# An attention and feed-forward kernel on one core: another order of the same 782 steps

## The chip, the core and the metric

The kernel runs on one core of a Trainium2 chip. The metric is the device time of one execution in microseconds; smaller is better. The core's engines work side by side and each takes its own instructions in program order: PE (TensorE: matmuls, with its weight loads listed as PEld), DVE (VectorE), ACT (ScalarE), POOL (GpSimd) and SP (SyncE, used here to issue transfers). They wait for each other through semaphores. Transfers are carried out by 16 DMA engines that all queues share.

## The reference

Eight batches of eight heads go through a softmax on both sides of an attention without a score matrix, and the result goes through a feed-forward part in which two up products are multiplied with each other:

```python
q_s = exp(q - max(q, -1)); q_s = q_s / (sum(q_s, -1) + 1e-9)        # over the 64 columns of a head
k_s = exp(k - max(k, 2));  k_s = k_s / (sum(k_s, 2) + 1e-9)         # over the 576 rows
attn = q_s @ (k_s^T @ v)                                            # q, k, v: 8 x 8 x 576 x 64, float32
x = attn.transpose(0, 2, 1, 3).reshape(4608, 512)
out = ((x @ w1) * (x @ w2) @ w3) @ w_out                            # w1, w2: 512 x 1024; w3: 1024 x 1024; w_out: 1024 x 512
```

## The kernel before, in words

The two last weights are multiplied once (`w3 @ w_out`, "the fold"), and the 4608 tokens go through the up products and one down product in chunks. Each batch gives a chunk of 512 tokens (numbers 0 to 7); the 64 tokens that are left of each batch of 576 are gathered into a ninth chunk, number 8.

Every piece of work is a named step, put into a plan with the engine or engines that can do it and a function that issues its instructions. Names are `kind.batch.part` or `kind.chunk.part`. Those that matter here:

- **Loads** (line 304): `w3.0` to `w3.7`, `wo.0`, `wo.1`, `w1.*`, `w2.*`, and `k`, `q`, `v` of batches 0 and 1 are issued by POOL, the others by SP. The first load on SP behind `q.0.1`, which is `q.2`, waits for the third load from the end of POOL's (line 328).
- **Fillers** `zero.N/count` (line 253): matmuls on zeros, whose result nobody reads.
- **Fold**: `w3t` turns a part of `w3` on PE (line 336), `w3T` copies it out of the PSUM bank (line 222), `pf` multiplies it with `w_out` on PE (line 346), `W3O` scales the result into SBUF (line 226).
- **k side** of a batch: `kmx` and `cb` (the maximum over rows, on DVE), `ksub` (line 416), `kexp` (ACT, line 424), `vc` (a copy of `v` to half precision, on ACT or POOL, line 222), `kv` (PE, line 442; in batches 0 and 1 in two halves) and `kv2` (DVE, line 460 on).
- **q side**: `qmx` (DVE, line 479), `qsub` (line 485), `qexp` (ACT, line 493), `qsm` (DVE, line 511), `qeps` (lines 517 and 518), `qrc` (DVE, line 522), `qn` (line 529). The result is turned by PE in batch 0 (`qt`, line 554, copied out by `qT`), and in the others by a transposing transfer on SP (`qd`, line 563).
- **Attention output**: `xm` and `xt` (PE, line 581) give the main part and the 64 tokens that are left; `xs` and `xts` scale them into the chunk's input (lines 226 and 228).
- **Feed-forward** of chunk c: `up.1.c.s.u` and `up.0.c.s.u` (PE, line 725: x times a part of `w2`, and of `w1`), `bs` (a copy of the first out of its bank, line 222), `ab` (DVE, line 740: the product of the two), `down` (PE, lines 747 and 762), `os` (a copy out, line 222), `st` (a store, issued by SP, lines 755 and 773).

A string `ORDER` (lines 64 to 132) lists all steps once. The plan issues them in this order, so each engine's own queue is the list with the other engines' steps left out. Where a step can go to more than one engine, the ending says which: `/A` ACT, `/D` DVE, `/P` POOL; behind a `zero` it is the number of matmuls. Data dependences become waits by themselves, and so does storage: PSUM has eight banks and a step that takes one waits for the step that empties its last use; the copies `osb`, `bsb` and others rotate over a few buffers too.

One more wait is written by hand. Steps on DVE and POOL that use the port that the two share are chained in list order whenever the engine changes:

```python
            if s["port"] and eng != "ACT" and held and i <= twos[-1] and held[0] != eng:
                link(got[0], held[1])
            if s["port"] and eng != "ACT":
                held = eng, got[-1]
```

Of the kernel before, what the change touches and what calls it, by code (L numbers as in the profile page):

```python
# [89 lines left out]
st.0.2 st.1.2 qd.3.1 k.5 v.4 qsm.4.0 qeps.4.0/A qmx.4.1 ab.2.0.2 up.1.2.0.3 up.0.2.0.3 up.1.2.0.4 up.0.2.0.4  # L90
up.1.2.0.5 up.0.2.0.5 up.1.2.0.6 bs.2.0.5/A bs.2.0.3/A ab.2.0.3 bs.2.0.4/A bs.2.0.6/A ab.2.0.5 ab.2.0.4
up.0.2.0.6 ab.2.0.6 up.1.2.0.7 up.0.2.0.7 vc.3.0/A bs.2.0.7/A qmx.5.1 st.1.3 vc.3.1/P v.5 kv.3 ab.2.0.7
down.2.0 kv2.3 xm.3.1 xm.3.0 qsub.4.1/P qexp.4.1 qsm.4.1 xs.3.1.0/D qrc.4.0 os.2.0/A xt.2 xs.3.0.0/A down.2.1
qsub.5.1/P xs.3.0.1/A xs.3.1.1/A down.2.2 os.2.2/A xts.2.1/A kmx.4.0 q.6 qeps.4.1/D st.2.2 qrc.4.1 down.2.3
# [5 lines left out]
up.0.3.0.7 xt.3 kv.4 ab.3.0.6 qexp.5.0 qeps.5.1/A ksub.5.0/P v.6 ab.3.0.7 down.3.0 down.3.1 kexp.5.0 os.3.0/A  # L100
k.7 xts.3.0/A os.3.1/A kmx.6.1 kv2.4 xts.3.1/A down.3.2 qrc.5.1 qmx.6.0 xm.4.0 os.3.2/A q.7 st.2.1 xs.4.0.0/A
xm.4.1 xs.4.0.1/A vc.5.1/P kv.5 qsub.6.0/P qn.5.1/P down.3.3 kmx.6.0 cb.6 ksub.6.1/D kv2.5 xs.4.1.1/A
xs.4.1.0/A up.1.4.0.0 up.0.4.0.0 bs.4.0.0/A up.1.4.0.1 st.3.0 qd.5.1 v.7 os.3.3/A st.3.3 st.3.2 vc.6.1/A
bs.4.0.1/A up.0.4.0.1 up.1.4.0.2 ksub.6.0/P ab.4.0.0 qsm.5.0 qmx.6.1 up.0.4.0.2 up.1.4.0.3 up.0.4.0.3
bs.4.0.2/A kexp.6.1 bs.4.0.3/D ab.4.0.2 qeps.5.0/A qrc.5.0 ab.4.0.1 qn.5.0/P qd.5.0 ab.4.0.3 up.1.4.0.4
bs.4.0.4/A up.0.4.0.4 up.1.4.0.5 up.0.4.0.5 up.1.4.0.6 bs.4.0.5/D qexp.6.0 ab.4.0.5 qsm.6.0 ab.4.0.4
qeps.6.0/D bs.4.0.6/A up.0.4.0.6 ab.4.0.6 qrc.6.0 qn.6.0/P qsub.6.1/P up.1.4.0.7 bs.4.0.7/A up.0.4.0.7
ab.4.0.7 down.4.0 down.4.1 down.4.2 os.4.0/A kexp.6.0 qexp.6.1 kmx.7.1 qmx.7.0 st.3.1 qmx.7.1 os.4.1/D
os.4.2/A xt.4 xts.4.1/D xts.4.0/A st.4.0 qd.6.0 vc.6.0/P xm.5.0 kv.6 xm.5.1 kv2.6 qsub.7.0/P xs.5.0.0/A
xs.5.0.1/A xs.5.1.1/A down.4.3 os.4.3/A qsub.7.1/P xs.5.1.0/D up.1.5.0.0 up.0.5.0.0 qsm.6.1 qeps.6.1/D qrc.6.1  # L110
kmx.7.0 qn.6.1/P bs.5.0.0/D ab.5.0.0 qd.6.1 st.4.1 st.4.2 vc.7.0/A up.1.5.0.1 up.0.5.0.1 cb.7 up.1.5.0.2
bs.5.0.2/A up.0.5.0.2 ab.5.0.2 bs.5.0.1/A ab.5.0.1 up.1.5.0.3 ksub.7.1/P bs.5.0.3/A qexp.7.1 up.0.5.0.3
up.1.5.0.4 up.0.5.0.4 up.1.5.0.5 bs.5.0.5/A up.0.5.0.5 qexp.7.0 qsm.7.1 qeps.7.1/A ab.5.0.3 ab.5.0.5
bs.5.0.4/D ab.5.0.4 kexp.7.1 up.1.5.0.6 bs.5.0.6/A vc.7.1/P up.0.5.0.6 ab.5.0.6 qrc.7.1 ksub.7.0/P kexp.7.0
# [5 lines left out]
up.0.6.0.3 up.1.6.0.4 bs.6.0.4/D up.0.6.0.4 up.1.6.0.5 st.4.3 ab.6.0.4 up.0.6.0.5 up.1.6.0.6 st.5.1 st.5.3  # L120
bs.6.0.3/D ab.6.0.3 bs.6.0.5/A ab.6.0.5 bs.6.0.6/D up.0.6.0.6 up.1.6.0.7 ab.6.0.6 up.0.6.0.7 bs.6.0.7/A
ab.6.0.7 down.6.0 up.1.7.0.0 down.6.1 bs.7.0.0/A os.6.0/D os.6.1/A up.0.7.0.0 ab.7.0.0 up.1.7.0.1 bs.7.0.1/A
up.0.7.0.1 up.1.7.0.2 up.0.7.0.2 up.1.7.0.3 bs.7.0.3/D up.0.7.0.3 up.1.7.0.4 up.0.7.0.4 ab.7.0.3 bs.7.0.2/D
ab.7.0.1 ab.7.0.2 up.1.7.0.5 down.6.2 down.6.3 bs.7.0.4/A bs.7.0.5/A os.6.2/D up.0.7.0.5 ab.7.0.5 st.6.2
st.6.1 st.6.0 up.1.7.0.6 bs.7.0.6/A ab.7.0.4 up.0.7.0.6 ab.7.0.6 os.6.3/D up.1.7.0.7 up.0.7.0.7 bs.7.0.7/D
ab.7.0.7 down.7.0 down.7.1 down.7.2 os.7.2/A st.7.2 up.1.8.0.0 up.0.8.0.0 up.1.8.0.1 bs.8.0.1/D os.7.0/D
bs.8.0.0/A ab.8.0.0 down.7.3 os.7.3/A st.6.3 st.7.3 os.7.1/A st.7.1 up.0.8.0.1 up.1.8.0.2 up.0.8.0.2
up.1.8.0.3 up.0.8.0.3 bs.8.0.2/D ab.8.0.1 bs.8.0.3/A ab.8.0.3 up.1.8.0.4 st.7.0 up.0.8.0.4 up.1.8.0.5
up.0.8.0.5 up.1.8.0.6 bs.8.0.5/D ab.8.0.2 ab.8.0.5 bs.8.0.6/D bs.8.0.4/A ab.8.0.4 up.0.8.0.6 ab.8.0.6
# [739 lines left out]
```

## Time and profile before

| | us |
|---|---|
| median of three runs | 236.59 |
| lowest and highest run | 236.57 and 237.1 |
| the profiled execution's own time | 236.66 |
| its span, from the first to the last instruction | 234.9 |
| what lies around the span | 1.8 |
| PE busy | 227.2 (97% of the span) |
| DVE busy | 184.0 (78%) |
| ACT busy | 114.7 (49%) |
| POOL busy | 110.4 (47%) |
| mean granted clock of PE | 0.998 of full speed |

How to read the rows that follow. A row of the chain of waits has a start in us from the span's start, a length, and the engine and line (or the transfer) that the end of the span hung on in that time. A row of the timeline has a start, a length (of all merged instructions), the engine, line and operation, what is written and read with the shape, how many instructions were merged, and in brackets the idle time in front of the first one and what ended it. Instructions overlap a little at their ends, so the distance between two starts is often shorter than a length. SPq and POOLq stand for the issuing of transfers. Lines that two steps share, such as 222, are those of a helper; the names of the tiles tell the steps apart.

### The profile page before, as it was taken

To read this page: it belongs to the slowest core of one execution; us is meant where nothing else is said; L and a number is where in the kernel's file an instruction comes from. 1 tells how busy PE (TensorE), PEld (TensorE's weight loads), DVE (VectorE), ACT (ScalarE), POOL (GpSimd) and SP (SyncE) were. 2 spreads that over 40 slices of the span, in tenths; PEclk is the share of its full clock that TensorE was granted. 3 is DMA by queue.
4 is the path that set the end of the run, shared out by engine and by line. 5 is a ranking of instruction groups with operands and counts; after the bars stand their busy time and mean duration, and the time that the engine had idled before them with its cause. 6 is when DMAs were issued, how large, how long until landed. Compare 5 with 4: busy or idle time off the path is not lost.

```text
span 234.9 us, 4814 instructions
## 1 busy us (share of the span) xinstructions
PE 227.2 (97%) x1928; PEld 120.2 (51%) x1928; DVE 184.0 (78%) x310; ACT 114.7 (49%) x180; POOL 110.4 (47%) x74
## 2 busy tenths in 40 slices
...
GB/s 226 215 299 217 307 250 265 379 290 273 393 320 200 325 264 196 377 399 262 290 338 355 258 170 79 38 125 16 99 174 39 0 3 0 134 13 142 71 45 134
DMA packets 38214, 46.84 MB, mean 199 GB/s; under 512 B 18352, under 2 KB 21680, under 8 KB 38192
## 3 DMA queue, kind: packets, MB, share of 16 engines
...
q14 instruction: 7, 0.06, 0.1%
...
## 4 chain that ended last, share of the span: by engine, by line
PE 89%; DMA 9%; POOL 1%; issue 0%; ACT 0%; POOLq 0%; ACTq 0%
PE pab L725 53%; PE po L747 24%; DMA w<-in_moe_w_dram 5%; DMA wosb<-in_moe_w_out_dram 3%; PE pf L346 3%; PE po L762 3%; PE pkv L442 2%; PE xm L581 2%; POOL w L304 1%; PE w3t L336 1%; PE xt L581 0%; PE pkv L451 0%; ACT osb L222 0%; POOL ident masks.py:199 0%; PE zero L253 0%
## 5 line engine op out<-in xcount | busy, mean ns | idle before, releaser
L725 PE MATMUL pab<-x,w2sb 128*128 128x512 f16 (+1 forms) x320 | 65.0, 336 | 0.0
L725 PE MATMUL pab<-x,w1sb 128*128 128x512 f16 (+1 forms) x320 | 64.9, 337 | 0.0
L740 DVE TENSOR_TENSOR ab<-pab,bsb 128x512 f16<-128x512 f32 x72 | 47.6, 681 | 15.7 <-PE pab L725 14.6
L747 PE MATMUL po<-W3O,ab 128*128 128x512 f16 x256 | 58.5, 379 | 0.0
L222 ACT CAST bsb<-pab 128x512 f16<-128x512 f32 x54 | 31.0, 585 | 47.7 <-PE pab L725 43.1
L725 PEld LDWEIGHTS <-w2sb 128*128 128x128 f16 x352 | 34.5, 98 | 28.4
L725 PEld LDWEIGHTS <-w1sb 128*128 128x128 f16 x352 | 34.3, 98 | 28.1 <-issue 0.2
L747 PEld LDWEIGHTS <-ab 128*128 128x128 f16 x256 | 24.2, 98 | 28.7 <-issue 0.8
L416 POOL TENSOR_TENSOR k<-k,cb 128x1152 f32<-128x1152 f32 x12 | 31.5, 2628 | 14.2 <-DVE k L416 8.3
L222 ACT COPY osb<-po 128x512 f32<-128x512 f32 (+1 forms) x28 | 15.9, 579 | 42.8 <-PE po L747 30.9
L529 POOL TENSOR_TENSOR en<-eq,qr 128x1280 f16<-128x1280 f16 (+1 forms) x13 | 27.8, 2139 | 16.4 <-DVE qr L522 13.6
L377 DVE TENSOR_REDUCE km<-k 128x128 f32<-128x1152 f32 x14 | 30.5, 2186 | 0.0
L485 POOL TENSOR_TENSOR q<-q,qm 128x1280 f32<-128x1280 f32 (+1 forms) x13 | 27.7, 2140 | 4.7 <-DVE qm L479 4.7
L222 DVE CAST bsb<-pab 128x512 f16<-128x512 f32 x18 | 12.3, 683 | 16.3 <-PE pab L725 16.2
L479 DVE TENSOR_REDUCE qm<-q 128x16 f32<-128x1024 f32 (+2 forms) x16 | 21.3, 1335 | 3.1 <-DMA q<-in_q_dram 2.9
L493 ACT ACTIVATE eq<-q 128x1024 f16<-128x1024 f32 (+2 forms) x16 | 18.7, 1167 | 9.6 <-DVE q L485 7.4
L424 ACT ACTIVATE ek<-k 128x1152 f16<-128x1152 f32 x16 | 18.6, 1163 | 6.4 <-POOL k L416 5.2
L511 DVE TENSOR_REDUCE qr<-eq 128x16 f32<-128x1024 f16 (+2 forms) x16 | 21.3, 1338 | 0.0
L346 PE MATMUL pf<-wosb,w3T 128*128 128x512 f16 x64 | 15.2, 380 | 1.4 <-ACT w3T L222 1.4
L226 ACT ACTIVATE x<-xm 128x512 f16<-128x512 f32 x25 | 13.2, 606 | 1.4 <-PE xm L581 1.4
L222 DVE COPY osb<-po 128x512 f32<-128x512 f32 (+1 forms) x9 | 5.9, 654 | 6.7 <-PE po L747 2.8
L346 PEld LDWEIGHTS <-w3T 128*128 128x128 f16 x64 | 5.7, 98 | 8.0 <-ACT w3T L222 2.3
...
## 6 DMA issues: line engine op xcount, KB each, us to landing
...
q<-in_q_dram SPq DMA_DIRECT2D x6, 1152.0 KB, 10.3
k<-in_k_dram SPq DMA_DIRECT2D x6, 1152.0 KB, 5.9
v<-in_v_dram SPq DMA_DIRECT2D x6, 1152.0 KB, 8.6
...
k<-in_k_dram POOLq DMA_DIRECT2D x1, 1152.0 KB, 14.1
```

The source lines that it names most:

```text
L222: return [(nc.scalar.copy if eng == "ACT" else engine[eng].tensor_copy)(out=out, in_=in_)]
L346: nc.tensor.matmul(st["pf", ft], lhsT=st["w3T", ft][:, gt, :], rhs=wosb[:, gt, :], start=(gt == 0), stop=(gt == N_FT - 1))
L377: dve.tensor_reduce(out=st["km", b][:, two(hp), :], in_=kb[:, two(hp), :, :].rearrange("p h j d -> p h d j"), axis=AX.X, op=ALU.max)
L416: return [engine[eng].tensor_tensor(out=kb[:, two(hp), :, :], in0=kb[:, two(hp), :, :], in1=st["cb", b][:, two(hp), None, :].broadcast_to( ...
L479: dve.tensor_reduce(out=st["qm", b][:, hs, j], in_=qb[:, hs, j, :], axis=AX.X, op=ALU.max, **({"negate": True} if (b, p) in FEXP else {}))
L485: return [engine[eng].tensor_tensor(out=qb[:, hs, j, :], in0=qb[:, hs, j, :], in1=st["qm", b][:, hs, j, None].broadcast_to([P, nh, n, D]), ...
L493: nc.scalar.activation(out=st["eq", b, p], in_=qb[:, hs, j, :], func=AF.Exp)
L511: dve.tensor_reduce(out=st["qr", b][(slice(None), *part(p))], in_=st["eq", b, p], axis=AX.X, op=ALU.add)
L529: return [engine[eng].tensor_tensor(out=st["en", b][:, j, hs, :].rearrange("p j h d -> p h j d"), in0=st["eq", b, p], in1=st["qr", b][:, h ...
L725: nc.tensor.matmul(st["p", one, c, sub, u][:, a * (t1 - t0):(a + 1) * (t1 - t0)], lhsT=w[:, ct, fb * P:(fb + 1) * P], rhs=x()[:, ct, t0:t1 ...
L740: dve.tensor_tensor(out=st["ab", c][:, nf * u:nf * u + nf, t0:t1], in0=cut(st["p", 0, c, sub, u]), in1=cut(st["bsb", c, sub, u]), op=ALU.mult)
L747: nc.tensor.matmul(st["po", c, tb], lhsT=st["ab", c][:, ft, tb * P:(tb + 1) * P], rhs=W3O[:, ft, :], start=(ft == 0), stop=(ft == N_FT - 1))
```

## The change

Only the list is another. The set of 782 names is the same, and no instruction is written differently; what changes is the place of most steps in their queues, the engine of some (their endings), and how many filler matmuls each `zero` issues. The part of the diff up to the third batch's `kv`, and two later lines:

```diff
 ORDER = """
-zero.0 zero.4/1 q.0.0 qmx.0.0 q.0.1 qmx.0.1 qsub.0.0/D qexp.0.0 qsub.0.1/D ident w3.3 w3t.3 w3.4 zero.3/6
-w3t.4 zero.5/1 zero.1/3 qsm.0.0 qeps.0.0/D qexp.0.1 qsm.0.1 w3T.3/A w3T.4/A wo.0 pf.3.0 pf.4.0 wo.1 pf.3.1
-w3.6 w3t.6 qrc.0.0 qn.0.0/D qeps.0.1/D qrc.0.1 qn.0.1/D qt.0.0.4 qt.0.1.0 pf.4.1 w3T.6/D qt.0.1.4 qT.0.0.4/A
-W3O.4/A W3O.3/A k.0.1 kmx.0.1 w3.0 k.0.0 pf.6.0 w3t.0 w3T.0/D qt.0.0.0 pf.6.1 W3O.6/A pf.0.0 qT.0.1.0/D w3.5
-w3t.5 w3T.5/A qT.0.1.4/A w3.7 pf.0.1 zero.6/1 w3t.7 w3T.7/A qT.0.0.0/A w3.2 w3t.2 pf.5.0 W3O.0/A pf.7.0 pf.7.1
-pf.5.1 w3.1 w3t.1 kmx.0.0 cb.0 ksub.0.0/D kexp.0.0 ksub.0.1/D v.0 kv.0.0 kexp.0.1 kv.0 W3O.5/D w3T.1/A w3T.2/D
-W3O.7/D kv2.0 pf.2.0 pf.2.1 W3O.2/A xm.0.0 xm.0.1 xs.0.1.1/A k.1 kmx.1.0 cb.1 pf.1.0 pf.1.1 xs.0.0.0/A
-xs.0.0.1/A w2.0 up.1.0.0.0 w2.1 q.1.0 qmx.1.0 bs.0.0.0/D qsub.1.0/D xs.0.1.0/A ksub.1.1/D up.1.0.1.0
-up.1.0.0.1 zero.2/1 up.1.0.1.1 bs.0.1.0/A bs.0.0.1/A W3O.1/A qexp.1.0 w1.0 up.0.0.0.0 up.0.0.0.1 ab.0.0.1
-qsm.1.0 up.0.0.1.1 up.0.0.1.0 w2.2 up.1.0.1.3 up.1.0.1.2 q.1.1 w1.1 v.1 ksub.1.0/P qmx.1.1 ab.0.0.0 ab.0.1.0
-bs.0.1.1/A kexp.1.1 bs.0.1.3/A qeps.1.0/A bs.0.1.2/A ab.0.1.1 up.1.0.0.2 up.1.0.0.3 bs.0.0.2/A up.0.0.0.2
-ab.0.0.2 qrc.1.0 qsub.1.1/P bs.0.0.3/A up.0.0.0.3 ab.0.0.3 up.0.0.1.3 ab.0.1.3 qexp.1.1 qsm.1.1 qn.1.0/P
-up.0.0.1.2 ab.0.1.2 kexp.1.0 vc.1.1/P qeps.1.1/D down.0.0 down.0.1 os.0.1/A vc.1.0/P kv.1.0 kv.1 q.2 qmx.2.0
-qrc.1.1 qn.1.1/P qmx.2.1 qsub.2.1/P k.2 os.0.0/A down.0.2 os.0.2/A xt.0 kv2.1 qd.1.0 xm.1.0 down.0.3
-xs.1.0.1/A xs.1.0.0/A xts.0.0/A up.1.1.0.0 up.0.1.0.0 qexp.2.1 xts.0.1/A kmx.2.0 v.2 kmx.2.1 cb.2 qsub.2.0/P
-qexp.2.0 up.1.1.0.1 bs.1.0.1/A os.0.3/A up.0.1.0.1 ab.1.0.1 bs.1.0.0/A ab.1.0.0 qsm.2.0 qd.1.1 q.3 up.1.1.0.2
-xm.1.1 up.0.1.0.2 up.1.1.0.3 up.0.1.0.3 xs.1.1.1/A xs.1.1.0/A qeps.2.0/A bs.1.0.2/A st.0.1 vc.2.0/P qsm.2.1
-bs.1.0.3/A qeps.2.1/A up.1.1.1.0 ksub.2.0/P st.0.0 ab.1.0.2 qrc.2.0 qn.2.0/P up.0.1.1.0 up.1.1.1.1 ab.1.0.3
-bs.1.1.0/A kexp.2.0 qrc.2.1 qn.2.1/P up.0.1.1.1 up.1.1.1.2 up.0.1.1.2 ksub.2.1/P up.1.1.1.3 qmx.3.1 ab.1.1.0
-bs.1.1.2/A ab.1.1.2 qmx.3.0 vc.2.1/A bs.1.1.3/A bs.1.1.1/A k.3 kmx.3.1 ab.1.1.1 kexp.2.1 qsub.3.0/P down.1.0
-down.1.1 os.1.0/A os.1.1/A up.0.1.1.3 q.4 qmx.4.0 xt.1 kv.2 xts.1.0/D ab.1.1.3 qexp.3.0 qsub.4.0/P qsub.3.1/P
-down.1.2 os.1.2/A qd.2.0 qd.2.1 kv2.2 xm.2.1 xts.1.1/D xs.2.1.0/A xm.2.0 xs.2.0.0/A xs.2.0.1/A qsm.3.0
...
-up.1.3.0.4 bs.3.0.4/A up.0.3.0.4 up.1.3.0.5 bs.3.0.3/A bs.3.0.5/A k.6 qn.4.0/P qd.4.0 st.2.0 ab.3.0.3 ab.3.0.4
...
-xs.6.0.1/A qn.7.1/P kv.7 xm.6.1 xt.6 kv2.7 qsm.7.0 down.5.1 down.5.2 down.5.3 qeps.7.0/D qrc.7.0 xs.6.1.1/D
...
+zero.0 q.0.0 qmx.0.0 zero.6/3 qsub.0.0/D q.0.1 ident w3.4 w3t.4 w3T.4/A qexp.0.0 w3.3 w3t.3 zero.1/1 zero.4/1
+qmx.0.1 qsub.0.1/D qexp.0.1 wo.0 pf.4.0 qsm.0.0 qeps.0.0/A w3T.3/D zero.2/1 pf.3.0 wo.1 pf.4.1 pf.3.1 W3O.3/A
+W3O.4/A qsm.0.1 qeps.0.1/D qrc.0.1 qrc.0.0 w3.0 w3t.0 w3T.0/A zero.5/1 qn.0.1/D qn.0.0/D qt.0.0.0 qt.0.1.4
+qT.0.0.0/D qt.0.0.4 qt.0.1.0 k.0.1 kmx.0.1 qT.0.0.4/D w3.6 w3t.6 w3T.6/A qT.0.1.4/A qT.0.1.0/A zero.3/1 k.0.0
+kmx.0.0 cb.0 ksub.0.0/D pf.0.0 pf.0.1 w3.5 w3t.5 w3T.5/A W3O.0/A pf.6.0 pf.6.1 W3O.6/A w3.7 w3t.7 w3.2 w3t.2
+w3T.7/A pf.5.0 pf.5.1 pf.7.0 pf.7.1 kexp.0.0 ksub.0.1/D kexp.0.1 w3T.2/D W3O.5/D W3O.7/D w3.1 w3t.1 v.0 kv.0.0
+kv.0 kv2.0 w3T.1/D pf.2.0 pf.2.1 W3O.2/A xm.0.0 xs.0.0.0/A xm.0.1 xs.0.1.1/A pf.1.0 k.1 kmx.1.0 cb.1
+ksub.1.1/D xs.0.0.1/A xs.0.1.0/A pf.1.1 W3O.1/A w2.1 up.1.0.0.1 w2.0 up.1.0.1.1 bs.0.0.1/D w1.0 up.1.0.0.0
+bs.0.0.0/A up.1.0.1.0 bs.0.1.0/A up.0.0.0.1 up.0.0.1.1 up.0.0.0.0 up.0.0.1.0 q.1.0 qmx.1.0 bs.0.1.1/A w2.2
+up.1.0.1.2 ab.0.0.1 ab.0.0.0 ab.0.1.0 q.1.1 qmx.1.1 w1.1 v.1 ksub.1.0/P kexp.1.0 ab.0.1.1 bs.0.1.2/D
+qsub.1.0/P kexp.1.1 qexp.1.0 up.1.0.0.3 up.1.0.0.2 up.1.0.1.3 bs.0.0.2/A up.0.0.0.2 up.0.0.0.3 qsub.1.1/P
+up.0.0.1.3 bs.0.0.3/A up.0.0.1.2 qsm.1.0 qeps.1.0/D qrc.1.0 ab.0.0.2 qexp.1.1 ab.0.0.3 down.0.0 down.0.1
+bs.0.1.3/A qsm.1.1 qeps.1.1/A ab.0.1.2 qrc.1.1 q.2 qmx.2.1 qmx.2.0 k.2 vc.1.0/A kv.1.0 vc.1.1/A os.0.0/A
+qn.1.0/P kv.1 ab.0.1.3 down.0.2 os.0.1/A xt.0 kv2.1 qd.1.0 xm.1.0 os.0.2/A qn.1.1/P qd.1.1 v.2 xts.0.0/A
+xs.1.0.1/A xs.1.0.0/A down.0.3 up.1.1.0.0 up.0.1.0.0 qsub.2.1/P qexp.2.1 xts.0.1/A qsub.2.0/P up.1.1.0.1
+up.0.1.0.1 up.1.1.0.2 qexp.2.0 kmx.2.0 kmx.2.1 cb.2 ksub.2.0/P ksub.2.1/P bs.1.0.1/A bs.1.0.0/A ab.1.0.0
+os.0.3/A vc.2.1/A xm.1.1 up.0.1.0.2 up.1.1.0.3 xs.1.1.1/A bs.1.0.2/D ab.1.0.1 xs.1.1.0/A up.0.1.0.3 up.1.1.1.0
+up.0.1.1.0 qsm.2.1 qsm.2.0 qeps.2.0/A bs.1.1.0/A up.1.1.1.1 bs.1.0.3/A up.0.1.1.1 q.3 qmx.3.0 ab.1.0.2
+ab.1.1.0 q.4 st.0.1 k.3 st.0.2 st.0.0 qrc.2.0 qn.2.0/P qeps.2.1/A bs.1.1.1/A qrc.2.1 ab.1.0.3 qn.2.1/P
+ab.1.1.1 qsub.3.0/P up.1.1.1.2 up.0.1.1.2 up.1.1.1.3 up.0.1.1.3 kexp.2.0 kexp.2.1 vc.2.0/A kv.2 qmx.3.1
+qmx.4.1 qsub.4.1/P bs.1.1.3/A ab.1.1.3 qd.2.0 bs.1.1.2/A kv2.2 qexp.3.0 ab.1.1.2 kmx.3.0 kmx.3.1 down.1.0
...
+qexp.5.1 vc.4.0/A ab.3.0.2 qsm.5.1 qsm.5.0 up.0.3.0.3 bs.3.0.3/A ab.3.0.3 up.1.3.0.4 bs.3.0.4/A up.0.3.0.4
...
+up.0.5.0.4 up.1.5.0.5 bs.5.0.5/A up.0.5.0.5 up.1.5.0.6 ab.5.0.3 ab.5.0.4 qn.7.1/D kexp.7.0 bs.5.0.6/A kexp.7.1
...
 """
```

The loads that SP and POOL issue, taken out of the list from the first on, with what SP does between them:

```
POOL before: w3.3 w3.4 wo.0 wo.1 w3.6 k.0.1 w3.0 k.0.0 w3.5 w3.7 w3.2 w3.1 v.0 k.1 w2.0 w2.1 q.1.0 w1.0 w2.2 q.1.1 w1.1 v.1
POOL after:  w3.4 w3.3 wo.0 wo.1 w3.0 k.0.1 w3.6 k.0.0 w3.5 w3.7 w3.2 w3.1 v.0 k.1 w2.1 w2.0 w1.0 q.1.0 w2.2 q.1.1 w1.1 v.1
SP before:   q.0.0 q.0.1 q.2 k.2 qd.1.0 v.2 qd.1.1 q.3 st.0.1 st.0.0 k.3 q.4 qd.2.0 qd.2.1 k.4 st.0.3 v.3 q.5
SP after:    q.0.0 q.0.1 q.2 k.2 qd.1.0 qd.1.1 v.2 q.3 q.4 st.0.1 k.3 st.0.2 st.0.0 qd.2.0 qd.2.1 k.4 v.4 v.3 st.0.3 q.5
```

More of the change, by code (lines that the diff above doesn't have):

```diff
@@ L85 @@
-down.1.1 os.1.0/A os.1.1/A up.0.1.1.3 q.4 qmx.4.0 xt.1 kv.2 xts.1.0/D ab.1.1.3 qexp.3.0 qsub.4.0/P qsub.3.1/P
-down.1.2 os.1.2/A qd.2.0 qd.2.1 kv2.2 xm.2.1 xts.1.1/D xs.2.1.0/A xm.2.0 xs.2.0.0/A xs.2.0.1/A qsm.3.0
-xs.2.1.1/A qeps.3.0/A kmx.3.0 qrc.3.0 qn.3.0/P down.1.3 os.1.3/A cb.3 ksub.3.1/P qexp.3.1 qsm.3.1 k.4 st.0.3
-v.3 q.5 st.1.0 qd.3.0 up.1.2.0.0 bs.2.0.0/A up.0.2.0.0 up.1.2.0.1 bs.2.0.1/A up.0.2.0.1 up.1.2.0.2 up.0.2.0.2
-qexp.4.0 qeps.3.1/A bs.2.0.2/A kexp.3.1 ab.2.0.1 qrc.3.1 ab.2.0.0 ksub.3.0/P kmx.4.1 kexp.3.0 st.1.1 qn.3.1/P
@@ L90 @@
[L90 to L94, printed above, removed]
@@ L95 @@
-up.1.3.0.0 cb.4 os.2.3/A bs.3.0.0/A os.2.1/D xts.2.0/A up.0.3.0.0 qn.4.1/P ksub.4.1/P up.1.3.0.1 qexp.5.1
-bs.3.0.1/A vc.4.0/P kmx.5.1 kexp.4.1 ab.3.0.0 ksub.4.0/P kmx.5.0 up.0.3.0.1 up.1.3.0.2 ab.3.0.1 bs.3.0.2/A
-vc.4.1/A up.0.3.0.2 up.1.3.0.3 up.0.3.0.3 qmx.5.0 ab.3.0.2 cb.5 st.2.3 qsub.5.0/P qd.4.1 kexp.4.0 qsm.5.1
-up.1.3.0.4 bs.3.0.4/A up.0.3.0.4 up.1.3.0.5 bs.3.0.3/A bs.3.0.5/A k.6 qn.4.0/P qd.4.0 st.2.0 ab.3.0.3 ab.3.0.4
-up.0.3.0.5 ab.3.0.5 up.1.3.0.6 up.0.3.0.6 vc.5.0/A bs.3.0.6/A up.1.3.0.7 bs.3.0.7/A ksub.5.1/P kexp.5.1
@@ L100 @@
[L100 to L114, printed above, removed]
@@ L120 @@
[L120 to L129, printed above, removed]
@@ new lines @@
+ab.1.1.0 q.4 st.0.1 k.3 st.0.2 st.0.0 qrc.2.0 qn.2.0/P qeps.2.1/A bs.1.1.1/A qrc.2.1 ab.1.0.3 qn.2.1/P
+ab.1.1.1 qsub.3.0/P up.1.1.1.2 up.0.1.1.2 up.1.1.1.3 up.0.1.1.3 kexp.2.0 kexp.2.1 vc.2.0/A kv.2 qmx.3.1
+qmx.4.1 qsub.4.1/P bs.1.1.3/A ab.1.1.3 qd.2.0 bs.1.1.2/A kv2.2 qexp.3.0 ab.1.1.2 kmx.3.0 kmx.3.1 down.1.0
+os.1.0/A down.1.1 down.1.2 os.1.1/A os.1.2/A qd.2.1 xm.2.0 xm.2.1 xt.1 xs.2.0.1/D xs.2.0.0/A xs.2.1.1/A
+xs.2.1.0/A qsub.3.1/P xts.1.0/A qexp.3.1 xts.1.1/A down.1.3 cb.3 ksub.3.0/P ksub.3.1/P up.1.2.0.0 up.0.2.0.0
@@ new lines @@
+bs.2.0.0/A qsm.3.0 qeps.3.0/A k.4 v.4 v.3 st.0.3 q.5 qsm.3.1 kmx.4.1 qeps.3.1/A qrc.3.1 qn.3.1/P qd.3.1 st.1.2
+up.1.2.0.1 up.0.2.0.1 bs.2.0.1/A ab.2.0.1 os.1.3/A up.1.2.0.2 up.0.2.0.2 up.1.2.0.3 ab.2.0.0 qrc.3.0
+bs.2.0.2/A bs.2.0.3/A up.0.2.0.3 ab.2.0.3 kmx.4.0 ab.2.0.2 up.1.2.0.4 up.0.2.0.4 qexp.4.1 bs.2.0.4/A kexp.3.1
+vc.3.1/P qn.3.0/P vc.3.0/A qd.3.0 ab.2.0.4 up.1.2.0.5 qmx.5.0 kexp.3.0 k.5 up.0.2.0.5 up.1.2.0.6 bs.2.0.6/A
+bs.2.0.5/A up.0.2.0.6 st.1.3 up.1.2.0.7 st.1.1 ab.2.0.6 ab.2.0.5 up.0.2.0.7 st.1.0 v.5 kv.3 bs.2.0.7/A
```

43 lines of the change are left out of this document (37 added, 6 removed).

## The prediction

> **What bounds the kernel now.** I read the chain of waits in order of time first, then busy time by stretch, then what PE itself waited for. Rows of the chain (start in us, length, engine and line):
>
> ```profile
> 11.13 12.19 DMA w<-in_moe_w_dram
> ...
> 23.37 0.70 PE w3t L336 x8
> 24.08 3.45 PE pf L346 x16
> ...
> 36.31 0.22 PE zero L253
> ...
> 56.11 4.37 PE pab L725 x40
> 60.48 0.34 PE xm L581 x8
> 60.82 8.84 PE pab L725 x80
> ...
> 224.80 6.94 PE po L762 x40
> ```
>
> Up to 23.32 the chain is a load: `w3.2`, issued at 11.13 and landed 12.19 later. From 23.37 to 231.74 every piece of it is PE work, laid end to end. Busy time by stretch (us busy and, in brackets, instructions, for PE, PEld, DVE, ACT, POOL; then clock and DMA):
>
> ```profile
> 23.40:60.00 36.60, 36.60 (x459) 25.87 (x460) 34.42 (x62) 22.87 (x36) 19.74 (x13) 1.00 1.16 296
> 60.00:128.00 68.00, 68.00 (x678) 36.04 (x676) 65.03 (x113) 48.72 (x78) 55.09 (x26) 1.00 1.03 308
> 128.00:165.00 37.00, 37.00 (x344) 17.49 (x343) 33.23 (x59) 19.85 (x31) 23.36 (x12) 1.00 0.56 122
> ```
>
> PE is busy in all of 23.40 to 165, at full clock. DVE is busy for 65.03 of 68.00 us up to 128: it is the second limit, with 3 us to spare. What PE waited for after its first matmul, all before 23.4 (us in total, times, longest):
>
> ```profile
> PE pf L346 <- ACT w3T L222: 1.4, 1, 1.4
> PE w3t L336 <- DMA w<-in_moe_w_dram: 1.1, 2, 0.6
> PE qtp L554 <- DVE en L529: 0.4, 1, 0.4
> ```
>
> So a new list can win very little: only what lies ahead of 23.37, and PE work that does nothing. It can lose anywhere, since PE runs its list in order and each step that comes late stops all of it.
>
> **What the change does to the sum.** No step is added or taken away. The 782 names are the same, so PE has the same matmuls, except the fillers `zero.1` to `zero.6`: 13 matmuls become 8. By the endings in the diff some steps change engine. `vc` on POOL goes from 8 to 4 (the rest to ACT), `qeps` on DVE from 7 to 2, `xts` on DVE from 6 to 2, `xs` from 7 to 4, `os` from 9 to 6; `bs` on DVE rises from 18 to 22. ACT takes most of this, and the fullest engine beside PE gets lighter.
>
> *Loads.* The POOL queue has the same sizes in the same places: `w3.3`/`w3.4`, `w3.0`/`w3.6` and `w2.0`/`w2.1` swap, and `w1.0` goes one place ahead of `q.1.0`. `w3.2` stays eleventh, so it lands at 23.32 again. Cost 0. The up products of the first chunk use the swapped `w2` part first, so they follow the swap.
>
> *The start.* PE must have done all its work ahead of `w3t.2` by 23.32. The rows from which the new order can be added up, of PE, ACT, DVE, and PE again:
>
> ```profile
> 7.14 0.71 PE L336 MATMUL w3t<-ident,w 128*128 128x128 f16 x8 [0.60 <-DMA w<-in_moe_w_dram]
> ```
> ```profile
> 8.55 2.43 ACT L493 ACTIVATE eq<-q 128x1152 f16<-128x1152 f32 x2 [6.32 <-DVE q L485]
> 10.88 1.91 ACT L222 COPY w3T<-w3t 128x1024 f16<-128x1024 f16 x2
> ```
> ```profile
> 14.55 1.36 DVE L529 TENSOR_TENSOR en<-eq,qr 128x1152 f16<-128x1152 f16 x1
> 15.83 0.68 DVE L222 COPY w3T<-w3t 128x1024 f16<-128x1024 f16 x1
> ```
> ```profile
> 18.21 0.65 PE L336 MATMUL w3t<-ident,w 128*128 128x128 f16 x8
> 18.69 0.39 PE L554 MATMUL qtp<-ident,en 128*128 128x128 f16 x4
> 18.91 1.89 PE L346 MATMUL pf<-wosb,w3T 128*128 128x512 f16 x8
> 20.64 0.65 PE L336 MATMUL w3t<-ident,w 128*128 128x128 f16 x8
> 21.12 1.03 PE L346 MATMUL pf<-wosb,w3T 128*128 128x512 f16 x4
> 21.99 0.38 PE L253 MATMUL zero<-zero 128*128 128x512 f16 x1
> ```
>
> Two things are new. ACT copies `w3T.4` ahead of `qexp.0.0`: from 7.85 (7.14 + 0.71) for 0.96 (half of 1.91) to 8.81, instead of an exp at 8.55, so +0.26. DVE copies `w3T.3` between the two `qsm`: +0.68. `qeps.0.0` leaves DVE, worth some 0.2 by the gap between short rows; I do not count it. The last `qn`, done at 15.91 (14.55 + 1.36), comes at 16.85, and it is now `qn.0.0`, for which the first of the four `qt` groups waits. Behind it PE has, by distances of starts in the last fence, 18 turns (4 in 0.22, so 1.0), three `w3t` (0.48 each), a filler (0.21) and 16 `pf` matmuls (8 in 1.73, so 3.46): 6.1, to 22.96. That is 0.36 ahead of `w3.2`. Cost 0, hidden by that load. Below nothing is excluded: the load bounds it. Above: with the modelled lengths (0.65, 1.89) instead of distances it would be 23.8, which is +0.5. I take the distances, because PE ran these very rows that way.
>
> *The filler at 36.31.* `zero.2` stood inside the first up products and moves to the start, where PE waits anyway: -0.22. Nothing takes its place on the path, because `w1.0`, which the next products need, is issued one place sooner. If a bank or `w1.0` stopped PE there after all, the gain would be 0.
>
> *`v.2`, moved behind `qd.1.1` on SP.* SP's rows:
>
> ```profile
> 48.29 1.33 SPq L563 DMA_TRANSPOSE qT<-en  x1
> 49.73 0.52 SPq L304 DMA_DIRECT2D v<-in_v_dram  x1
> 53.71 1.37 SPq L563 DMA_TRANSPOSE qT<-en  x1
> 55.19 0.67 SPq L304 DMA_DIRECT2D q<-in_q_dram  x1
> ```
>
> `v.2` went out at 49.73, between the two turns; now it takes the place of `q.3`, 1.48 behind the second. `qrc.1.1` now stands ahead of the two `qmx.2`, so `qn.1.1` and this turn can come up to 1.4 earlier (one such reduction), none later: `v.2` goes out at 53.8 to 55.2. How long to land (the one row is `q.3`, the other all loads of `v`, min/median/max):
>
> ```profile
> q<-in_q_dram SPq DMA_DIRECT2D x1, 1152.0 KB, 7.9
> ```
> ```profile
> DMA to landing us min/median/max: 6.6/9.0/16.8
> ```
>
> `q.3` had `v.2` in front of it and took 7.9; now nothing but turns is in front, so I take the shortest, 6.6: 60.4 to 61.8, middle 61.1; with 7.9, up to 63.1. Who waits: ACT has `vc.2.1` next, and behind it `xs.1.1.1` and `xs.1.1.0`, which `up.1.1.1.0` needs. That starts, by the chain, at 56.11 + 4.37 + 0.34 + three groups of 0.88 - 0.22 = 63.2. ACT's rows:
>
> ```profile
> 60.87 1.09 ACT L226 ACTIVATE x<-xm 128x512 f16<-128x512 f32 x2 [0.48 <-PE xm L581]
> ```
> ```profile
> 64.94 1.17 ACT L424 ACTIVATE ek<-k 128x1152 f16<-128x1152 f32 x1
> 67.95 0.58 ACT L222 CAST bsb<-pab 128x512 f16<-128x512 f32 x1 [1.84 <-PE pab L725]
> 68.43 1.16 ACT L222 CAST v<-v 128x1152 f16<-128x1152 f32 x1
> ```
>
> Copy and two scalings take 1.16 + 1.09 = 2.25, so `v.2` has to be there by 61.0. The middle costs +0.1; the ends are 0 and +2.1.
>
> By the Trainium skill's page "DMA: Bandwidth & Descriptors", section "Latency and other measured facts", a transposing DMA reaches 261 GB/s; the two turns (8 and 10 blocks of 128 x 128 in two bytes, 256 and 320 KB) would then be estimated at 1.0 and 1.2 us, `v.2` would be there before 61 and cost 0, and the rival on it would fall. The trace speaks against it: the stretch around the second turn took `q.3` 7.9 us.
>
> *`kv.2`, 3.9 us earlier on PE.* It now stands ahead of `down.1.0`, eight groups behind the start of `up.1.1.1.0`: 63.2 + 7.1 = 70.3. ACT has, from the end of `up.1.1.1.1` (63.2 + 3 x 0.88 = 65.9): `bs.1.1.1`, `kexp.2.0`, `kexp.2.1`, `vc.2.0`, which is 0.58 + 2 x 1.17 + 1.16 = 4.08, to 70.0. Margin 0.3, cost 0; if the `v.2` place slips, PE slips with it. From below 0; above, each us that ACT is late is one of PE, bounded by the 2.1 above.
>
> *DVE ahead of chunk 3.* Up to `ab.3.0.3`, whose bank `up.0.3.0.7` needs, DVE's queue from `cb.2` on gains one `qsm` (a pass over 1024 elements) and a `bs`, and loses small ones: about 1.1 us more. It is covered by the idle time that ends in this row, which the new order fills:
>
> ```profile
> 68.89 0.69 DVE L740 TENSOR_TENSOR ab<-pab,bsb 128x512 f16<-128x512 f32 x1 [1.81 <-PE pab L725]
> ```
>
> Cost 0; with that cover gone, up to +1.1. *After 128* DVE was idle 3.77 of 37.00 us and gets lighter. The new wait for the shared port is `qn.7.1/D` behind `ksub.7.1/P`; the `ab.5` products queue behind it, and their up products take PE until the end of the chunk. Cost 0.
>
> Sum: the profiled execution's own 236.66 (0.07 above the median of 236.59 shown) + 0 - 0.22 + 0.1 = 236.54, so 236.5.
>
> **Rivals.** *A late `v.2`.* Place: `vc.2.1` on ACT, in front of `xs.1.1`. It decides from a landing of about 62 on, 1 us behind its due time. For it: the margin by the rows is nil, and a median landing (9.0) would be worse still. Against it: fewer bytes are in front than `q.3` had. At 63.1: 236.44 + 2.1 = 238.5; at 62: 237.4. *Several small margins give way*: 0.36 at the start, 0.3 at `kv.2`, DVE's 1.1. One in full is +0.5 to +1.1: 237.0 to 237.6. For it: DVE is over 95% busy. Against: DVE has less to do. *A gain beyond the filler.* The start can give no more than the load does; if all eleven loads came 0.36 sooner, PE would be just in time: 236.44 - 0.36 = 236.1. Against: same bytes in the same places. *The list does nothing*: the filler gave its 0.22 to a wait for a bank: 236.7.
>
> **How the numbers follow.** 0.3% is 0.7 us, about what a measurement of this kernel can tell from no change: faster means below 235.9, slower above 237.3. Forecast (236.2 to 237.0), with the list that does nothing: 0.50. Late `v.2`: 0.24, of which 0.23 slower. Small margins: 0.17, of which 0.11 slower, the rest same. Further gain: 0.09, of which 0.06 below 235.9. So faster 0.06, same 0.60, slower 0.34. The range for 8 in 10 is 236.0 to 238.3: it takes in the late landing up to nearly 63 and leaves the rest out; the forecast's own is 236.2 to 237.0.
>
> **What would show it.** `w3t.2` at 23.3 to 23.4, with PE idle in front of it: right; at 23.6 or later with none: the start was mis-sized. No `zero` row after 24. `up.1.1.1.0` at 63.2 with no wait for ACT: `v.2` was in time; a PE wait on `xs` there, with ACT's cast waiting for `in_v`: the first rival. `kv.2` within 0.3 of 70.3. No PE wait behind 23.4 over 0.3. A span over 235.6, or any PE wait above 0.7, makes the forecast wrong.

## The result, and the profile after

| | before | after |
|---|---|---|
| median of 11 runs each, same chip | 236.82 us | 237.76 us |
| lowest and highest run | 236.43 and 237.72 | 237.19 and 239.72 |
| the profiled execution's own time | 236.66 | 237.55 |
| its span | 234.9 | 235.8 |
| filler matmuls beyond `zero.0` | 13 | 8 |

After stands to before as 1.0048, with an interval of 1.0032 to 1.0063: slower by 0.9 us, and the single runs lie over 2.5 us, where before they lay over 1.3. The forecast of 236.5 is missed by 1.3 us. The range of 236.0 to 238.3 holds the median, but by luck: its upper part stood there for a late `v.2`, which did not come. Both signs that the prediction named for being wrong came: the span is over 235.6, and PE has a wait above 0.7.

The chain of waits of the changed kernel (start, length, what):

```profile
11.00 12.31 DMA w<-in_moe_w_dram
...
23.35 0.71 PE w3t L336 x8
...
33.68 13.97 PE pab L725 x128
47.65 3.45 PE po L747 x16
...
60.59 9.71 PE pab L725 x88
70.31 0.71 PE pkv L442 x72
...
76.85 0.06 PE xt L581 x8
...
123.98 12.96 PE pab L725 x60
...
148.10 3.38 issue
151.48 0.04 POOL k L416
151.52 1.90 issue
153.42 3.26 POOLq L864
...
156.71 1.49 DVE en L529
158.19 1.62 issue
159.81 1.28 DVE ab L740 x2
161.09 0.61 DVE bsb L222
...
161.79 0.70 DVE ab L740
...
162.54 0.39 PE po L747
...
225.69 6.94 PE po L762 x40
```

Up to 124 the chain is again a load and then PE alone, and it is ahead of the one before. There chunk 4 began here:

```profile
73.98 0.19 PE xt L581 x8
74.17 0.74 PE pkv L442 x72
...
124.53 13.81 PE pab L725 x64
```

So the changed list is 0.55 ahead at 124 (123.98 against 124.53) and 0.89 behind at the last step (225.69 against 224.80). It lost 1.44 in between, and behind the start PE waited in only one place:

```profile
PE po L747 <- DVE ab L740: 1.0, 2, 0.8
```

That is `down.5.0` waiting for the last `ab.5.0` products. The timeline of PE gives the loss in full: `down.5.0` starts at 159.69, its eight matmuls should take 1.73 (as in the prediction's rows of such a group), to 161.42, and the next step starts at 162.86, 1.44 later.

```profile
159.69 1.24 PE L747 MATMUL po<-W3O,ab 128*128 128x512 f16 x5
161.15 0.60 PE L747 MATMUL po<-W3O,ab 128*128 128x512 f16 x2 [0.21 <-DVE ab L740]
162.54 0.39 PE L747 MATMUL po<-W3O,ab 128*128 128x512 f16 x1 [0.79 <-DVE ab L740]
162.86 0.26 PE L581 MATMUL xt<-qT,kv 64*64 64x64 f16 x8
```

Why the products are late shows in the timelines of POOL and DVE:

```profile
151.48 5.20 POOL L416 TENSOR_TENSOR k<-k,cb 128x1152 f32<-128x1152 f32 x2 [3.39 <-issue]
156.64 1.90 POOL L529 TENSOR_TENSOR en<-eq,qr 128x1024 f16<-128x1024 f16 x1
```
```profile
150.90 0.45 DVE L412 STREAM_TRANSPOSE cb<-mxe 128x256 f32<-128x256 f32 x1
...
156.71 3.18 DVE L529 TENSOR_TENSOR en<-eq,qr 128x1280 f16<-128x1280 f16 x1 [0.46 <-POOL k L416]
159.81 1.28 DVE L740 TENSOR_TENSOR ab<-pab,bsb 128x512 f16<-128x512 f32 x2
```

`qn.7.1` on DVE takes 3.18 us here. The chain cuts it into 1.49 of work and 1.62 of "issue", time for which it has no cause. The two rows side by side have one: POOL starts `qn.7.0` at 156.64, DVE starts `qn.7.1` 0.07 later, POOL is done at 158.54, and DVE 1.35 after that. The hand-written chain of the port should have kept the two apart. It does not: `link` is called only up to the last DVE step of the chain (`i <= twos[-1]`). In the list before, that was `qn.7.0/D`, behind all POOL steps. In the changed list it is `qn.7.1/D`, and `qn.7.0/P` stands behind it, free to start as soon as POOL is.

The other "issue" of the chain, 3.38 ahead of `ksub.7.0`, is no riddle either: `cb.7`, which it needs, ends on DVE at 151.35 (150.90 + 0.45).

### The profile page after: what moved, and what is told of

The parts are those of the page before. It is cut to its first block, busy times and chain, and to the rows that moved or that the text cites. A ratio compares the mean times of both kernels' runs of the same rounds, so it can differ in the third digit from the quotient of the medians.

```text
span 235.8 us, 4798 instructions
## 1 busy us (share of the span) xinstructions
PE 227.2 (96%) x1923; PEld 119.9 (51%) x1923; DVE 181.2 (77%) x298; ACT 118.7 (50%) x194; POOL 109.7 (47%) x72
## 4 chain that ended last, share of the span: by engine, by line
PE 78%; DMA 9%; DVE 5%; issue 4%; POOLq 1%; ACT 1%; POOL 1%; ACTq 0%; DVEq 0%
PE pab L725 47%; PE po L747 20%; DMA w<-in_moe_w_dram 5%; DMA wosb<-in_moe_w_out_dram 3%; PE pf L346 3%; PE po L762 3%; PE pkv L442 2%; PE xm L581 2%; DVE qr L511 2%; POOLq L864 1%; DVE km L377 1%; DVE ab L740 1%; DVE en L529 1%; POOL w L304 1%; PE w3t L336 1%
## 5 line engine op out<-in xcount | busy, mean ns | idle before, releaser
L222 ACT CAST bsb<-pab 128x512 f16<-128x512 f32 x50 | 28.1, 589 | 34.5 <-PE pab L725 34.4
L222 ACT COPY osb<-po 128x512 f32<-128x512 f32 (+1 forms) x31 | 17.6, 581 | 48.8 <-PE po L747 41.4
L416 POOL TENSOR_TENSOR k<-k,cb 128x1152 f32<-128x1152 f32 x13 | 33.9, 2622 | 17.4 <-DVE cb L412 7.6
L485 POOL TENSOR_TENSOR q<-q,qm 128x1024 f32<-128x1024 f32 (+1 forms) x14 | 29.6, 2125 | 7.7 <-DVE qm L479 4.5
L529 POOL TENSOR_TENSOR en<-eq,qr 128x1024 f16<-128x1024 f16 (+1 forms) x13 | 27.3, 2107 | 7.7 <-DVE qr L522 5.4
L222 DVE CAST bsb<-pab 128x512 f16<-128x512 f32 x22 | 14.9, 684 | 11.2 <-PE pab L725 11.0
L222 DVE COPY osb<-po 128x512 f32<-128x512 f32 (+1 forms) x6 | 3.9, 646 | 19.3 <-PE po L747 14.2
L226 ACT ACTIVATE x<-xm 128x512 f16<-128x512 f32 x28 | 15.6, 611 | 1.6 <-PE xm L581 1.6
L222 ACT CAST v<-v 128x1152 f16<-128x1152 f32 x10 | 11.4, 1153 | 0.1
```

The source lines that it names most:

```text
L222: return [(nc.scalar.copy if eng == "ACT" else engine[eng].tensor_copy)(out=out, in_=in_)]
L416: return [engine[eng].tensor_tensor(out=kb[:, two(hp), :, :], in0=kb[:, two(hp), :, :], in1=st["cb", b][:, two(hp), None, :].broadcast_to( ...
L485: return [engine[eng].tensor_tensor(out=qb[:, hs, j, :], in0=qb[:, hs, j, :], in1=st["qm", b][:, hs, j, None].broadcast_to([P, nh, n, D]), ...
L529: return [engine[eng].tensor_tensor(out=st["en", b][:, j, hs, :].rearrange("p j h d -> p h j d"), in0=st["eq", b, p], in1=st["qr", b][:, h ...
```

## The experiments

Each is compared with runs of the kernel before on the same chip (medians 236.75 to 236.93 there). In the first four the line numbers of the profile are five lower, since the list takes five lines less.

**e1_link: one wait more.**

```diff
-            if s["port"] and eng != "ACT" and held and i <= twos[-1] and held[0] != eng:
+            if s["port"] and eng != "ACT" and held and held[0] != eng:
```

> One wait is added to the changed kernel: POOL's qn.7.0 waits for DVE's qn.7.1, which stands ahead of it in the list. Theory A (the two multiplies of fp16 tiles meet: DVE's qn.7.1, 3.18 us in the trace, is held until POOL's qn.7.0 ends): qn.7.1 starts at about 156.7 and takes 1.4 to 1.5, ab.5.0.7 ends 1.7 us sooner, the stall of 1.4 inside down.5.0 goes, span 234.4, median 236.3 (237.76 - 1.44). Theory B (the price is the wait for ksub.7.1 with four DVE steps queued behind it, whatever POOL does next): qn.7.1 still takes about 3, stall 1.4, median 237.7. Theory C (the profile's stall is not what makes the median late: some landing, v.2 or the transposes ahead of xm.7, is): stall gone in the profile, yet the median stays above 237.

Measured: 236.64 (12 runs, 236.17 to 238.37), 1.0004 [0.9986, 1.0022] of before. DVE and POOL:

```profile
156.73 1.49 DVE L524 TENSOR_TENSOR en<-eq,qr 128x1280 f16<-128x1280 f16 x1 [0.34 <-POOL k L411]
158.38 1.29 DVE L735 TENSOR_TENSOR ab<-pab,bsb 128x512 f16<-128x512 f32 x2 [0.17 <-PE pab L720]
159.59 0.68 DVE L217 CAST bsb<-pab 128x512 f16<-128x512 f32 x1
160.37 0.69 DVE L735 TENSOR_TENSOR ab<-pab,bsb 128x512 f16<-128x512 f32 x1
```
```profile
158.35 1.91 POOL L524 TENSOR_TENSOR en<-eq,qr 128x1024 f16<-128x1024 f16 x1 [1.66 <-ACT bsb L217]
```

`qn.7.1` starts at the same time and takes 1.49 instead of 3.18; the last product ends at 161.06 instead of 162.48; PE has no wait behind the start, the span is 234.5 and the last step starts at 224.40. That the wait for `ksub.7.1` is still there and costs nothing fells theory B. The median falls by 1.1, not by 1.44, which the two intervals (some 0.4 us to either side each) do not tell apart. It is below the 237 of theory C, but single runs still reach 238.4, and something else must make those late.

**e2_behind: the multiply moved out of the way.** `qn.7.1/D` behind `ab.5.0.7`:

```diff
-... ab.5.0.4 qn.7.1/D kexp.7.0 ... bs.5.0.7/D ab.5.0.7 qn.7.0/P down.5.0
+... ab.5.0.4 kexp.7.0 ... bs.5.0.7/D ab.5.0.7 qn.7.1/D qn.7.0/P down.5.0
```

> qn.7.1/D moves behind ab.5.0.7 in the list, four DVE steps later; POOL is left as it is. Theory A: POOL's qn.7.0 (156.6 to 158.5) is over before DVE comes to qn.7.1, which then takes 1.4; ab.5.0.7 ends at about 159.9, no stall in down.5.0; median 236.3. The turn of qn.7.1 for xm.7 then has its data at about 161.3, still ahead of the 163.2 at which the first turn of that batch goes out now. Theory B: also no stall, 236.3, so this run tells A and B apart only together with the other two. Theory C: median stays above 237.

Measured: 237.16 (12 runs, 236.09 to 238.32), 1.0016 [1.0000, 1.0032]. The multiply takes 1.48 at 161.59 and `down.5.0` does not wait, so the stall is gone a second time. The median misses theory A's 236.3 and lies where theory C has it. (The last product ends at 161.67, 0.75 of that from the start, so about 1 us later than expected: DVE had waited 2.00 for an up product.) The profiled execution lost 0.75 at the start: its first up products begin at 34.43, not at 33.68. Busy time by stretch (PE, PEld, DVE, ACT, POOL; then granted clock, DMA share, GB/s):

```profile
7.00:9.00 2.00, 0.72 (x8) 0.58 (x8) 1.97 (x2) 0.34 (x1) 0.56 (x1) 1.00 1.13 221
9.00:11.00 2.00, 1.14 (x10) 0.74 (x11) 0.85 (x2) 2.00 (x3) 0.53 (x1) 1.00 1.05 211
11.00:13.00 2.00, 1.35 (x5) 0.55 (x5) 2.00 (x3) 1.09 (x2) 0.53 (x1) 0.77 1.04 206
13.00:15.00 2.00, 2.00 (x6) 0.67 (x5) 1.93 (x5) 0.00 (x0) 0.53 (x1) 0.50 1.08 321
15.00:17.00 2.00, 2.00 (x10) 0.88 (x8) 2.00 (x2) 0.00 (x0) 0.75 (x1) 0.88 1.09 293
```

PE was busy for 1.86 of the 4 us up to 11, since it waited for late loads, and then its clock fell to half. Twelve `pf` matmuls show what that costs, first here, then in the changed kernel's profile, where the clock stayed at 1.00 (that they also start later here comes from the load of `wo.0`, which landed at 11.60 instead of 10.72):

```profile
13.36 3.81 PE L341 MATMUL pf<-wosb,w3T 128*128 128x512 f16 x12
```
```profile
12.50 2.76 PE L346 MATMUL pf<-wosb,w3T 128*128 128x512 f16 x12 [0.51 <-DVE w3T L222]
```

The clock does not explain the median of this run. Of its seven executions over 237, only two (237.21 and 237.38) have a mean clock of 0.993 or less; the other five, up to 238.32, have it at 0.999 or 1.000, and what made them late is open.

**e3_order: a wait instead of the meeting.** `qn.7.0/P` ahead of `qn.7.1/D` in the list.

> qn.7.0/P goes ahead of qn.7.1/D in the list, so DVE's multiply now waits for POOL's by a semaphore instead of meeting it. Theory A (the meeting costs just the time until POOL's multiply ends): qn.7.1 starts at 158.6, takes 1.4, ends at 159.9 to 160.0 as it does now; stall 1.3 to 1.5; median 237.6 to 237.9. If the meeting costs more than waiting (both slowed), it is better: qn.7.1 ends before 159.6 and the median is 237.4 or lower. Theory B: the same as now.

Measured: 238.15 (4 runs), 1.0063 [1.0049, 1.0078], over the 237.9 expected; the two of the four with a mean clock of 0.993 are the highest. DVE, then POOL:

```profile
158.40 1.49 DVE L524 TENSOR_TENSOR en<-eq,qr 128x1280 f16<-128x1280 f16 x1 [2.31 <-POOL en L524]
159.81 1.28 DVE L735 TENSOR_TENSOR ab<-pab,bsb 128x512 f16<-128x512 f32 x2
```
```profile
156.45 1.91 POOL L524 TENSOR_TENSOR en<-eq,qr 128x1024 f16<-128x1024 f16 x1
```

The products start at 159.81, as in the changed kernel. That it is the same hundredth is chance, since POOL's multiply ends 0.18 sooner here (158.36 against 158.54): counted from that end, DVE is done after 1.53 with the semaphore and after 1.35 in the meeting. POOL's multiply takes 1.90 in the meeting and 1.91 without. So the meeting is no slowdown of both; DVE waits until POOL's instruction is over, as A has it.

**e4_front: the first 475 steps of the changed list, the rest in the old order.**

> The changed list up to the first up product of chunk 4 (475 of its 782 steps), then all that is left in the order of the list before. Theory A: the first part is 0.55 ahead of the kernel before (chunk 4's up products at 123.98 instead of 124.53), and the second has no meeting of the two multiplies: median 236.82 - 0.55 = 236.3. Theory C with v.2 or another landing of the first part: 237.2 or more, with runs near 239 as the changed kernel has. If the second part's order does not fit the state in which the first leaves the engines: a PE wait behind 124 in the profile, and 236.5 to 237.5.

Measured: 243.62 (4 runs), 1.0286. PE waited 4.9 for one `bs` of chunk 4, behind which ACT had waited 9.5 for a load of `v`. The two halves do not fit together, and the run says nothing on the first half's gain. Its profiled execution also lost the clock at the start: PE was busy for 1.88 of the 4 us up to 11, and the clock was 0.50 from 12.2 to 15.6.

**e5_warm: longer fillers at the start, with the added wait.**

```diff
-... w3.3 w3t.3 zero.1/1 zero.4/1 ...
+... w3.3 zero.1/6 w3t.3 zero.4/6 ...
```

> The kernel with the added wait (e1_link), and two fillers of the start made longer: zero.1 goes ahead of w3t.3 with 6 matmuls instead of 1 behind it, zero.4 has 6 instead of 1. PE computes 10 more filler matmuls while it waits for w3.3 and wo.0. Theory D (the runs of the changed list spread because PE is busy too little from 7 to 11 us: when the loads land 0.4 to 0.9 later, the granted clock falls to 0.50 at 13 to 15 us, as in the profile of e2_behind, and the first up products start at 34.4 instead of 33.7): clock 1.00 in all stretches from 9 to 30, first up products at 33.5 to 33.8, and the runs between 236.7 and 237.4 go back to 236.2 to 236.6; median 236.3. Theory E (the spread comes from late landings of v.7 or of the turns ahead of xm.7): no change, median 236.6, highest over 238.

Measured: 236.18 (12 runs, 235.82 to 238.46), 0.9987 [0.9969, 1.0005]; first up products at 33.66, clock 1.00 in every stretch up to 24, and PE's only wait behind its first matmul is 1.0 for a `qn` of batch 0. The median is theory D's; the spread is not, since three of 12 stay over 236.9.

**e6_cold: the kernel before, with short fillers.** `zero.3/6` becomes `/1`, `zero.1/3` becomes `/1`.

> The kernel before, with zero.3 cut from 6 matmuls to 1 and zero.1 from 3 to 1, so that its start has about as few fillers as the changed list has. Theory D: some executions lose the clock at the start: median 236.9 to 237.6 instead of 236.8, with a spread of 1 us or more; in the profile, if it catches one, a clock of 0.5 to 0.9 somewhere between 11 and 17 us and first up products 0.5 to 0.9 later than 33.7. Theory E: as before, 236.4 to 237.2.

Measured: 237.07 (11 runs, 236.51 to 237.31), 1.0010 [1.0001, 1.0019]. Its profiled execution caught the clock:

```profile
9.00:11.00 2.00, 0.72 (x7) 0.23 (x5) 2.00 (x2) 1.89 (x3) 0.34 (x1) 1.00 1.08 217
11.00:13.00 2.00, 0.97 (x5) 0.38 (x6) 1.93 (x5) 1.88 (x3) 0.53 (x1) 1.00 1.02 202
13.00:15.00 2.00, 2.00 (x7) 0.75 (x7) 1.93 (x4) 0.00 (x0) 0.61 (x2) 0.59 1.08 336
15.00:17.00 2.00, 2.00 (x15) 1.35 (x14) 1.00 (x1) 0.00 (x0) 1.27 (x2) 0.56 1.09 288
```

First up products at 34.44, 0.75 behind the 33.69 of before. Here the clock can be told from the loads: the twelve `pf` matmuls start only 0.10 later than in the kernel before (second row), and take 1.34 more.

```profile
12.03 4.15 PE L346 MATMUL pf<-wosb,w3T 128*128 128x512 f16 x12 [2.30 <-ACT w3T L222]
```
```profile
11.93 2.81 PE L346 MATMUL pf<-wosb,w3T 128*128 128x512 f16 x12 [1.44 <-ACT w3T L222]
```

The median lies in the ranges of both theories, and the spread is 0.80, not the 1 us of theory D. But the four executions with a mean clock of 0.993 or less took 237.22 to 237.31, and the median of the other seven is 236.83. Over all runs, the mean granted clock of an execution was 0.993 or less in 2 of 92 of the kernel before, in 4 of 11 of e6_cold, in 10 of 39 of those with the changed list's short fillers (the changed kernel, e1 to e3), and in 1 of 66 of those with the long ones (e5, e7 to e11); e4_front, all four of whose executions have it, is left out for its long wait further on. Theory D is right about the clock, though not about the spread.

**e7_loads: two transfers of batch 7 sooner.** e5_warm, with `v.7` behind `qd.5.1` (ahead of three stores) and `qd.7.1` ahead of `st.5.0`.

> e5_warm, with v.7 on SP ahead of three stores of chunk 3 (it goes out about 2 us sooner, at 138.7) and qd.7.1 ahead of st.5.0. Theory E: the runs above 237 go, highest under 237, median 0.1 to 0.4 below e5_warm. Theory D: the same as e5_warm within 0.1.

Measured: 236.42 (12 runs, 236.00 to 237.25), 0.9993 [0.9983, 1.0004]. The median is no better than that of e5_warm; the highest run is lower, but three of 12 stay over 237. Neither theory's numbers.

**e9_warm_only: the fillers without the added wait.**

> The changed list with the longer fillers of e5_warm alone, without the added wait. Theories A and D are of two separate places, so their prices add: down.5.0 still stalls 1.4 (qn.7.1 over 3 us in the profile), clock 1.00 at the start; median e5_warm's 236.18 + 1.1 to 1.4 = 237.3 to 237.6, against 237.76 of the changed kernel. If it comes out at 236.5 or less, the meeting of the two multiplies was not the price; at 237.8 or more, the fillers gain nothing by themselves.

Measured: 237.73 (12 runs, 237.33 to 240.20), 1.0047 [1.0026, 1.0068]. The meeting is back (PE waits 1.0 for `ab`), and against e5_warm the same one wait is worth 1.55. But the fillers gained nothing over the changed kernel's 237.76, so the two prices do not simply add. There was little to gain: only one of the changed kernel's 11 executions had the low clock. The profiled execution, 238.36, shows another loss; PE's rows are:

```profile
71.32 5.35 PE L747 MATMUL po<-W3O,ab 128*128 128x512 f16 x24
77.10 0.63 PE L581 MATMUL xm<-qT,kv 64*64 64x512 f16 x8 [0.43 <-DMA qT<-en]
```

It started 0.37 late (34.05), and `xm.2` waited 0.43 for a turn that took 5.46 to land. Both together are the 0.80 by which its last step starts later than the changed kernel's (226.49 against 225.69).

**e8_all: everything, with `qn.7.1/D` behind the products in place of the added wait.**

> e7_loads (fillers, v.7 sooner, qd.7.1 ahead of st.5.0, the added wait) with qn.7.1/D behind ab.5.0.7 in place of the added wait. If the rest of the spread (single runs of 237.0 to 238.5) comes from a late ksub.7 that holds qn.7.1 and with it the ab.5 products, it goes: highest under 237, median 236.1 to 236.3. If it comes from somewhere else, single runs over 237 stay, as in e7_loads (3 of 12).

Measured: 236.82 (12 runs, 235.91 to 237.96), 0.9997 [0.9978, 1.0016]. Six of 12 over 236.9: the rest of the spread does not come from a late `ksub.7`.

**e10_turns and e11_both: the turns of batch 2 sooner.** In e5_warm (e10) and e7_loads (e11):

```diff
-q.3 qmx.3.0 ab.1.0.2 ab.1.1.0 ... qrc.2.0 qn.2.0/P qeps.2.1/A bs.1.1.1/A qrc.2.1 ab.1.0.3 ...
+q.3 ab.1.0.2 qrc.2.0 qn.2.0/P ab.1.1.0 ... qeps.2.1/A bs.1.1.1/A qrc.2.1 qmx.3.0 ab.1.0.3 ...
```

> e5_warm (longer fillers, added wait), with qmx.3.0 on DVE moved behind qrc.2.1 and qrc.2.0 one product sooner. Theory F (the rest of the spread comes from the two turns of batch 2, which land with under 1 us to spare ahead of xm.2; the profiled execution of e9_warm_only waited 0.4 for one that took 5.5 to land): POOL's two multiplies of batch 2 start at 65.3 instead of 66.9, the turns go out 1.6 sooner, and the runs over 236.8 become rarer than in e5_warm (3 of 12); median 236.0 to 236.2. If the spread has another source, 3 or more of 12 stay over 236.8. A wait of PE for ab.1.1.0's bank or for qexp.3 would make it slower: 236.5 or more.

> e10_turns with v.7 sooner and qd.7.1 ahead of st.5.0 (the two edits of e7_loads). If the tail has two sources, the turns of batch 2 and the loads of batch 7, this is the one without runs over 236.8, median 236.0 to 236.2; if theory F is all, it is the same as e10_turns within 0.1.

Measured: e10_turns 236.50 (12 runs, 235.87 to 237.83), 0.9985 [0.9967, 1.0003]; four of 12 over 236.8, no fewer than e5_warm's three, so theory F does not hold as the source of the rest. e11_both 236.18 (6 runs, 235.84 to 236.71), 0.9961 [0.9947, 0.9976]: 0.4% faster than the kernel before, with none of its six runs over 236.8.

## Why the prediction was wrong

*The start: right.* `w3t.2` starts at 23.35 (forecast 23.3 to 23.4), `w3.2` lands 12.31 after its issue. PE came to it about 0.2 ahead, not 0.36: the group of turns in front starts at 22.62 and takes 0.48.

*The filler at 36.31: right in size.* `down.0` starts at 47.65 instead of 47.88, so 0.23 for the 0.22. What the sum left out is that fillers do something: with so few of them between the first folds, the clock fell in 10 of 39 executions. The profiled one was not among them, so its time does not hold this price, which was 0.75 at the start in the profiled executions of e2_behind and e6_cold. Nor does the median, since only one of the 11 executions has the low clock.

*`v.2` and `kv.2`: the cost was 0 and not 0.1.* `kv.2` starts at 70.31 (forecast 70.3), and PE has no wait there. ACT's row in the changed kernel is

```profile
60.24 1.15 ACT L222 CAST v<-v 128x1152 f16<-128x1152 f32 x1
```

with no wait, so `v.2` was there by 60.24, a little ahead of the 60.4 to 61.8 worked out. In e5_warm the same cast waited for it until 60.55, which is still in time. The rival of a late `v.2` fell.

*DVE ahead of chunk 3: right, 0.* PE has no wait there.

*A gain not seen.* 0.32 more up to 124: `xt.1` now stands behind `xm.2` and takes 0.06 of the path instead of 0.19, and three `kv` groups (of batches 2, 4 and 5) take 0.71, 0.67 and 0.64 instead of 0.74, 0.75 and 0.72. Why these became shorter was not tried.

*The step that failed* is the last: "The new wait for the shared port is `qn.7.1/D` behind `ksub.7.1/P`; the `ab.5` products queue behind it [...]. Cost 0." That wait was there and cost nothing (e1_link has it still). What it overlooked is the step on the other side of `qn.7.1/D`: the chain of the port ends with the list's last DVE step, the changed list has `qn.7.0/P` behind it, and the two multiplies start within 0.07 of each other. DVE stood still until POOL was done, the four DVE steps behind it came 1.4 late, and `down.5.0` with them.

With these in, the sum of the prediction comes out: 236.66 - 0.23 - 0.32 + 1.44 = 237.55, the profiled execution's own time.

*What stays open.* Runs of 237 to 240 that none of the edits removed for certain; most of them are at full clock. Whether the fillers gain anything in the median is open too: 0.46 with the added wait (e1 to e5), with intervals that overlap, and nothing without it (e9). The low clock is not the reason for the 0.46, since without its three low-clock executions the median of e1_link is 236.60. Late landings ahead of `xm.2` were seen to cost 0.4 once, but making room there did not narrow the spread in 12 runs. Part of the rest may lie at the start: in the profiled executions of e9_warm_only, e10_turns and e11_both the first up products begin at 34.05, 34.09 and 34.20, up to 0.5 late at full clock. This was not followed up.
